# Grouped bursts: scores between the two bursts of a head pair inside the up products

## The chip, the cores and the metric

The kernel runs on one core of a Trainium2 chip. The metric is the device time of one execution in microseconds (us), as the median of several executions.

## The reference, cut to what matters

Grouped-query attention over 8 batches of 384 rows (16 query heads, 4 key heads, head size 64), then a feed-forward block with a squared ReLU on the 3072 rows that the attention gives:

```python
scores = scale * np.matmul(q, k.transpose(0, 1, 3, 2))
attn = np.exp(scores - np.max(scores, axis=-1, keepdims=True))
attn = attn / (np.sum(attn, axis=-1, keepdims=True) + 1e-09)
x = np.matmul(attn, v)                 # heads side by side: 3072 x 1024
h = np.maximum(x @ w_in, 0.0)          # 1024 x 2048
out = (h * h) @ w_out                  # 2048 x 1024
```

## The kernel before, in words

The work goes batch by batch (384 rows each). TensorE is driven by one long list of pieces, and the program that writes the kernel plans the order of that list itself: a recorder (`Recorder`) keeps an estimated clock for each engine and an estimated end for each operation, and a planner loop asks at each step which pieces could start now. Each engine then executes its own list strictly in that order, with semaphore waits where operations depend on each other.

While the feed-forward block of one batch runs, the attention of the next batch is woven into it. Four kinds of pieces matter here:

- **Up pieces** (L927, in `zipped` and `strassen`, L836 and L868): from batch 2 on, x times w_in is done by a seven-product scheme (Strassen's, Winograd's form) on half-size blocks in fp16. A piece is eight matmuls of 192 columns, four in each 64-row half of the array. A batch has 28 units of four half pieces each. A finished unit is taken out of its PSUM bank (4 to 7) by DVE or ACT (L898 to L911), then scaled and squared by ACT and GpSimd (L812 to L824). In the planner an up piece is called "ffn".
- **Down pieces** (L971): h squared times w_out, in the same scheme; also "ffn". Their results leave PSUM by DVE or ACT into `y_sb` (L1126 to L1134, L1344) and go out on SP's DMA queue (L1351).
- **Pieces of scores** ("sc", `burst_small`, L464): two matmuls of 512 columns or four of 256 (L471), into one of the two pairs of banks (0, 1) and (2, 3), followed by one exponential on ACT (L481) into a slot of `expT`. There are 18 for a batch. From batch 3 on, `expT` has six slots for the twelve blocks of keys of a batch (L198), so later scores become allowed only when head pairs of outputs have been finished.
- **Outputs of a head pair** (`av_halves`, L525): eight pairs a batch, each in two bursts of 18 matmuls of 65 columns (L539), in one of the two pairs of banks. The first burst is "av", the second "av2". The second adds into the same banks from the opposite 64-row halves, and therefore waits for the first to complete; then DVE divides (L552, L554). After each second pair a DMA transpose on SP's queue (L559) turns the result into `xT`. When a batch has all of `xT`, DVE forms three sums and a difference (`sums`, L673, L682) that the up products need.

A stretch of up products and a stretch of down products alternate. The down stretch of batches 2, 4 and 6 is short (7 products), that of batches 3 and 5 long (14 products).

The changed loop (L1930 to L2030) plans everything from batch 2 on. In each round it makes a list of candidates, each a tuple of the estimated time at which it can start, a priority (lower goes first), its kind, and a flag that says whether its spacing is kept. Inside the up products (`inside`) the flag of outputs is set when at least `AV_IN` = 4 up pieces have passed since the last burst of either kind, and that of scores when `SC_LATE` = 2 pieces (for the next batch) or `SC_IN` = 8 pieces (for the one after) have passed since the last scores. Outside, one piece is enough. Then it picks:

```python
ready = [x for x in cand if x[3] and x[0] <= now] or [x for x in cand if x[0] <= now]
what = min(ready, key=lambda x: x[1]) if ready else min(cand)
```

So among the candidates that can start now, those whose flag is set come first; if there are none, any that can start now fills the gap; and if there is none either, the earliest is taken. An up piece always has its flag set. `upkeep` (L1697) places the work of the other engines between the pieces: loads, transposes, evictions, sums.

Of the kernel before, what the change touches and what calls it, by code (L numbers as in the profile page):

```python
# [171 lines left out]
def bass_gqa_attention__then__ffn_squared_relu_kernel(  # L172
# [32 lines left out]
    R = Recorder(nc)  # L205
# [1415 lines left out]
    ff = dict(b=0, tiles=list(range(EARLY, NFC)), now=[], down=downs(0), carry=None)  # L1621
# [41 lines left out]
    av_open = []  # L1663
    margin = 0.5
    since, AMONG = 9, 2
    AV_IN, SC_LATE, SC_IN = 4, 2, 8
    load_pieces, dma_at, pe_last, LOAD_GAP, TURN_GAP = [], [0.0], [], 2.0, 3.5

    BLOCK, EDGE = 128, 51
# [106 lines left out]
    while ff["b"] < SB:  # L1776
        now = R.clock["tensor"]
# [4 lines left out]
        cand = []  # L1782
        wait = 0.1 if split else 0.0
        if turn_q:
            b, g, w = turn_q[0]
# [5 lines left out]
        if av_q and len(av_open) < 1 + on_halves(av_q[0][0] - 1):  # L1791
            b, c = av_q[0]
# [12 lines left out]
        if sc_q:  # L1805
            b, u = sc_q[0]
# [15 lines left out]
            if ok:  # L1822
# [3 lines left out]
                t = max(R.when(reads=reads) + 1.5 * (b == 2 and u < 9), R.when(writes=[("bank", base + i) for i in range(2)]))  # L1826
                cand.append((t, 4 if beside or loose and b > SB else 2.5 if loose else 0, "sc"))
        early_banks[:] = [i for i in ((6, 7, 0, 1, 2, 3) if sc_q and sc_q[0] == (1, 0) else (6, 7)) if i not in held]
        for n, lane in enumerate(lanes):
            chunks, need, banks, _ = lane[0]  # L1830
            if x_done[0] >= chunks:
                t = R.when(reads=need)
                if banks is not None:
                    if not banks:
                        continue
                    t = max(t, open_bank(banks))
# [4 lines left out]
        if f_head is not None:  # L1841
            chunks, need, banks, piece, *swap = f_head
            if x_done[ff["b"]] >= chunks and not (held and banks and held & set(banks) and isinstance(banks, list)):
                t = max([R.when(reads=need)] + [x() for x in swap])
                if banks:
                    t = max(t, max(open_bank([i]) for i in banks) if isinstance(banks, list) else open_bank(banks))
# [10 lines left out]
        if not cand:  # L1857
            b = next_sum()
# [68 lines left out]
                R.clock["tensor"] += 0.0 if on_halves(ff["b"] - 1) else 0.1  # L1927
            ff_take(split)

    since_av, since_sc = 9, 9  # L1930
    while ff["now"] or ff["tiles"] or ff["down"]:
        now = R.clock["tensor"]
        upkeep(now)
# [12 lines left out]
                    t = max(t, max(open_bank([i]) for i in banks) if isinstance(banks, list) else open_bank(banks))  # L1946
                cand.append((t, 5, "ffn", True))
        if av_open:
            cand.append((R.ops[av_open[0][3]]["end"], 0, "av2", since_av >= (AV_IN if inside else 1)))
        if av_q and len(av_open) < 2:  # L1950
            b, c = av_q[0]
            needs = {(b, c // 2 * NJ + j, 3 * (c % 2) + t) for j in range(NJ) for t in range(3)}
            places = [p for p in PAIRS if not held & set(p)]
            if needs <= scored and b in measured and b <= ff["b"] + 1 and b - NXT not in tail_open and places:
                place = min(places, key=lambda p: max(open_bank([i]) for i in p))
                t = max(max(open_bank([i]) for i in place), R.when(reads=av_reads(b, c)))
                cand.append((t, 1, "av", since_av >= (AV_IN if inside else 1)))
        if spread_q:
            pair = min((p for p in PAIRS if not held & set(p)), key=lambda p: max(open_bank([i]) for i in p), default=None)
            if pair:  # L1960
# [1 line left out]
        if sc_q:  # L1962
            b, u = sc_q[0]
            pieces = later[u]
            tiles = {(b, x, t) for x, c0, n in pieces for t in range(c0 // 128, (c0 + n) // 128)}
            bases = [i for i in (0, 2) if not held & {i, i + 1}]
            if (turned >= b or (b, max(x for _, x, _ in tiles) // (NU // 2)) in turned_h) and b <= ff["b"] + 2 and not (inside and len(ff["now"]) <= 10 and b > ff["b"] + 1) and (b != LEAN or pairs >= 8 * b) and pairs // 2 * NJ + SLOTS[b] > b * NU + max(x for _, x, _ in tiles) and bases:
                base = min(bases, key=lambda i: max(open_bank([i + x]) for x in range(2)))
                t = max(R.when(reads=[r for p in pieces for r in score_reads(b, *p)]) + 3.0 * (b > SB + 1), max(open_bank([base + i]) for i in range(2)))
                cand.append((t, 3, "sc", since_sc >= ((SC_LATE if b == ff["b"] + 1 else SC_IN) if inside else 1)))  # L1970
        if not cand:
            if force():
                continue
# [10 lines left out]
        ready = [x for x in cand if x[3] and x[0] <= now] or [x for x in cand if x[0] <= now]  # L1984
        what = min(ready, key=lambda x: x[1]) if ready else min(cand)
        since_av = 0 if what[2] in ("av", "av2") else since_av + (what[2] == "ffn")
        since_sc = 0 if what[2] == "sc" else since_sc + (what[2] == "ffn")
        if what[2] == "av":
            b, c = av_q.pop(0)
# [56 lines left out]
```

## Time and profile before

| | |
|---|---|
| median of 3 runs | 394.03 us (393.51 to 394.4) |
| the profiled execution, its own time | 394.68 us |
| its span in the trace | 392.6 us |
| TensorE matmuls busy | 386.4 us (98%) |
| TensorE weight loads busy | 305.3 us (78%) |
| VectorE (DVE) busy | 309.0 us (79%) |
| ScalarE (ACT) busy | 272.1 us (69%) |
| GpSimd (POOL) busy | 143.6 us (37%) |

The profile is one execution; times in it are counted from the start of its span. PE is TensorE's matmul row, PEld its weight loads, which run beside the matmuls. Matmuls overlap, so the distance between two starts, and not the length of one, is what a matmul costs. A line of a group names the line of the kernel, the engine, the operation, output and inputs, the count, busy time and mean length, and the idle time ahead of it with what ended it. In the rows of waits the numbers are the total in us, the count and the longest. In the rows of windows they are the length of the stretch, and for each engine its busy time and (x) its number of instructions, then TensorE's clock, the share of the DMA engines and GB/s.

In this trace the five up stretches with outputs woven in run from about 128.9, 166.9, 218.2, 257.2 and 308.7 us; the short down stretches begin at about 152, 243 and 333 us.

### The profile page before, as it was taken

What the parts mean: (1) busy time and instruction counts of PE and PEld (TensorE: products, weight loads), DVE (VectorE), ACT (ScalarE), POOL (GpSimd) and SP (SyncE); (2) the same over time, 40 slices, a digit from 0 to 9 for tenths busy, and PEclk for the clock granted to TensorE, in tenths of its full rate; (3) what the DMA queues carried; (4) which work ended last, traced back from release to release, by engine and by line L of the source; (5) the groups of instructions that cost most, each with busy time, mean ns of one, the idle gap of its engine ahead of it and who ended that gap; (6) DMA issues with size and microseconds to landing.
All of it is one profiled execution on the core that took longest, in us unless ns stands there. A gap on an engine that the chain in (4) does not pass through costs nothing. (4 is left out here: it accounts for less than half of the span.)

```text
span 392.6 us, 15577 instructions
## 1 busy us (share of the span) xinstructions
PE 386.4 (98%) x6987; PEld 305.3 (78%) x6990; DVE 309.0 (79%) x645; ACT 272.1 (69%) x397; POOL 143.6 (37%) x167
## 2 busy tenths in 40 slices
PE   8899999999999999999999999999999999999997
PEld 6565674455555899899988999899988899899643
DVE  4589788899989988888886678797885688856642
ACT  6848998789845897868882587878782297435511
POOL 7765420044002563466422154526401145225210
PEclk9999999999999999999999999999999999999999
DMA  9999999996339875884798316877722222120013
GB/s 176 179 197 154 206 202 178 160 258 103 42 78 131 182 104 75 126 161 79 99 133 172 120 25 83 123 139 94 69 64 86 102 46 23 48 83 4 28 68 122
DMA packets 95635, 44.40 MB, mean 113 GB/s; under 512 B 75984, under 2 KB 89552, under 8 KB 95568
## 3 DMA queue, kind: packets, MB, share of 16 engines
q0 software_dynamic: 36672, 17.44, 35.7%
q1 hardware_dynamic: 58080, 25.39, 32.2%
q8 instruction: 55, 0.90, 1.0%
q10 hardware_dynamic: 816, 0.57, 0.5%
q14 instruction: 12, 0.10, 0.1%
HBM read 35.65 MB, written 12.58 MB: 123 GB/s over the span
## 5 line engine op out<-in xcount | busy, mean ns | idle before, releaser
L481 ACT ACTIVATE expT<-ps 128x1024 bf16<-128x1024 f32 (+1 forms) x124 | 121.1, 1015 | 24.7 <-PE ps L471 24.3
L971 PE MATMUL ps<-w_out_sb,h2T 64*128 64x512 f16 x512 | 94.5, 376 | 0.0
L927 PE MATMUL ps<-xT,w_in_sb 64*128 64x192 f16 x1152 | 84.3, 243 | 0.3 <-DVE y_sb L1134 0.2
L927 PEld LDWEIGHTS ps<-xT,w_in_sb 64*128 64x128 f16 x1152 | 70.5, 94 | 3.0 <-PE ps L927 0.7
L824 POOL TENSOR_TENSOR h2T<-hr 128x384 f16<-128x384 f32 x55 | 44.8, 835 | 53.7 <-ACT hr L812 53.6
L927 PE MATMUL ps<-s_all,wx 64*128 64x192 f16 x768 | 51.8, 242 | 0.0
L471 PE MATMUL ps<-qT,kT 64*128 64x256 bf16 (+2 forms) x336 | 51.3, 323 | 0.5 <-DVE qT L442 0.2
L812 ACT ACTIVATE hr<-hr,bits 128x384 f32<-128x384 f32 x72 | 42.6, 608 | 11.1 <-DVE hr L911 10.7
L971 PE MATMUL ps<-area,xT 64*128 64x512 f16 x256 | 50.1, 376 | 0.0
L971 PEld LDWEIGHTS ps<-w_out_sb,h2T 64*128 64x128 f16 (+1 forms) x512 | 38.0, 94 | 14.8 <-DVE hr L898 0.4
L911 DVE TENSOR_TENSOR hr<-ps,hr 128x384 f32<-128x384 f32 x72 | 39.3, 555 | 8.4 <-PE ps L927 5.1
L927 PEld LDWEIGHTS ps<-s_all,wx 64*128 64x128 f16 x768 | 43.7, 94 | 1.2
L1126 ACT ACTIVATE y_sb<-ps,bits 128x512 f32<-128x512 f32 (+2 forms) x23 | 15.3, 669 | 40.4 <-PE ps L971 31.2
L1134 DVE SCALAR_TENSOR_TENSOR y_sb<-ps,bits,y_sb 128x512 f32<-128x512 f32 (+1 forms) x36 | 26.3, 745 | 21.1 <-PE ps L971 13.2
L635 PE MATMUL ps<-xT,w_in_sb 64*128 64x384 bf16 x448 | 41.6, 323 | 0.4 <-DMA w_in_sb<-in_moe_w_in_dram 0.2
L539 PE MATMUL ps<-v_aug,expT 64*128 64x65 bf16 x1680 | 41.8, 190 | 0.1
L539 PEld LDWEIGHTS ps<-v_aug,expT 64*128 64x128 bf16 x1680 | 38.4, 94 | 1.9 <-DVE o_sb L554 0.3
L635 PEld LDWEIGHTS ps<-xT,w_in_sb 64*128 64x128 bf16 x448 | 22.2, 94 | 15.0 <-issue 1.3
L927 PE MATMUL ps<-xT,wx 64*128 64x192 f16 x384 | 32.6, 242 | 0.0
L927 PE MATMUL ps<-s_all,w_in_sb 64*128 64x192 f16 x384 | 32.5, 242 | 0.0
L971 PE MATMUL ps<-area,h2T 64*128 64x512 f16 x128 | 31.9, 376 | 0.0
L903 ACT COPY hr<-ps 128x384 f32<-128x384 f32 x33 | 15.5, 481 | 23.3 <-PE ps L927 22.7
(152 smaller groups left out, 746.1 us busy)
## 6 DMA issues: line engine op xcount, KB each, us to landing
out_dram<-y_sb SPq DMA_DIRECT2D x45, 256.0 KB, 2.5
w_in_sb<-in_moe_w_in_dram POOLq DMA_DIRECT2D x8, 512.0 KB, 15.1
w_out_sb<-in_moe_w_out_dram POOLq DMA_DIRECT2D x4, 1024.0 KB, 30.9
q_st<-in_q_dram POOLq DMA_DIRECT2D x19, 192.0 KB, 5.1
q_st<-in_q_dram POOLq DMA_DIRECT2D x4, 384.0 KB, 25.5
k_st<-in_k_dram POOLq DMA_DIRECT2D x6, 192.0 KB, 4.5
k_st<-in_v_dram POOLq DMA_DIRECT2D x5, 192.0 KB, 4.8
wx<-in_q_dram POOLq DMA_DIRECT2D x2, 384.0 KB, 6.7
```

The source lines that it names most:

```text
L471: mm = pe.matmul(ps[:, base + x, m * wide:(m + 1) * wide], kT[at(b)][64 * x:64 * x + 64, u, :], q_cols(b, u // NJ, x, c0, c0 + wide))
L481: R.add("scalar", lambda e: e.activation(dst, src, AF.Exp, scale=0.125), reads=keys, writes=[("expT", slot(b, u), t) for u, _, _ in pieces ...
L539: m = pe.matmul(ps[:, p[x], n * DP:n * DP + D + 1], w, v_aug[b % 2][r, g * NJ + j, 0:D + 1], start=(n + j + y == 0), stop=(n + j + y == 2 ...
L635: m = pe.matmul(bank(4 + xs[x])[:, 0:S], w_in_sb[r, kc, c * 128:(c + 1) * 128], xT[b % NXT][r, kc, :], start=(phase < 2 and kc == 0), stop ...
L812: R.add("scalar", lambda e, val=val, to=to: e.activation(val, val, AF.Relu, scale=to), reads=[("hr", r)] + by, writes=[("hr", r)], cost=0. ...
L824: n = R.add(eng, lambda e, dst=dst, two=two: e.tensor_tensor(dst, two, two, ALU.mult), reads=[("hr", r)], writes=keys, cost=0.77 if other ...
L903: R.add("scalar", lambda e: e.copy(hr[r][:, :], src), reads=[("bank", at)], writes=[("hr", r)], cost=0.45, after=hr_read.pop(r, ()))
L911: R.add("vector", lambda e: e.tensor_tensor(hr[r][:, :], src, hr[r][:, :], ALU.add), reads=[("bank", at), ("hr", r)], writes=[("hr", r)], ...
L927: return lambda pe: pe.matmul(bank(at)[:, f * h:f * h + h], w[r, kc, c:c + 128], m[r, kc, :], start=(prod in (1, 5, 2) and y + f + kc == 0 ...
L971: return lambda pe: pe.matmul(bank(p.at)[:, 0:512], p.a(k, r), p.w(k, r), start=start, stop=stop, skip_group_check=True)
L1126: R.add(eng, lambda e: e.activation(y_sb[y][:, c0:c1], bank(at)[:, c0:c1], AF.Copy, scale=gs[g]) if eng == "scalar" else e.tensor_scalar(y ...
L1134: R.add("vector", lambda e: e.scalar_tensor_tensor(y_sb[z][:, c0:c1], bank(at)[:, c0:c1], gs[g], y_sb[y][:, c0:c1], ALU.mult, ALU.add), re ...
```

## The change

Four edits in the planner loop, all for the time inside the up products:

- A first burst may start when five up pieces (`AV_GROUP`) have passed since the last burst, instead of four. A second burst keeps four, except in a group (below).
- The spacing of scores of the next batch is six up pieces instead of two.
- `lately` holds the kinds of the last two pieces. Right after a first burst, a piece of scores has its flag set whatever the spacing, if ACT's estimated clock is at most 1.2 us ahead, and it has priority over all else, if it can start within 0.3 us.
- Right after a first burst and a piece of scores, the second burst has its flag set whatever the spacing, and its estimated start is put 0.1 us earlier.

The computation stays the same; only the order of the pieces changes, and with it what the planner places between them.

```diff
-    AV_IN, SC_LATE, SC_IN = 4, 2, 8
+    AV_IN, AV_GROUP, SC_LATE, SC_IN = 4, 5, 6, 8
...
-    since_av, since_sc = 9, 9
+    since_av, since_sc, lately = 9, 9, ["ffn", "ffn"]
...
-            cand.append((R.ops[av_open[0][3]]["end"], 0, "av2", since_av >= (AV_IN if inside else 1)))
+            cand.append((R.ops[av_open[0][3]]["end"] - 0.1 * (lately == ["av", "sc"]), 0, "av2",
+                         since_av >= (AV_IN if inside else 1) or inside and lately == ["av", "sc"]))
...
-                cand.append((t, 1, "av", since_av >= (AV_IN if inside else 1)))
+                cand.append((t, 1, "av", since_av >= (AV_GROUP if inside else 1)))
...
-                cand.append((t, 3, "sc", since_sc >= ((SC_LATE if b == ff["b"] + 1 else SC_IN) if inside else 1)))
+                cand.append((t, -1 if lately[-1] == "av" and t <= now + 0.3 else 3, "sc", inside and lately[-1] == "av" and R.clock["scalar"] <= now + 1.2 or since_sc >= ((SC_LATE if b == ff["b"] + 1 else SC_IN) if inside else 1)))
...
         what = min(ready, key=lambda x: x[1]) if ready else min(cand)
         since_av = 0 if what[2] in ("av", "av2") else since_av + (what[2] == "ffn")
+        lately = [lately[-1], what[2]]
```

## The prediction

> **What bounds the kernel now.** I read the page's head first, then the clock row, then the waits of TensorE over the stretch in which the changed loop orders the work (128 to 346 us), then its timeline.
>
> ```profile
> span 392.6 us, 15577 instructions
> PE 386.4 (98%) x6987; PEld 305.3 (78%) x6990; DVE 309.0 (79%) x645; ACT 272.1 (69%) x397; POOL 143.6 (37%) x167
> ...
> PEclk9999999999999999999999999999999999999999
> ```
>
> ```profile
> PEld ps L927 <- PE ps L927: 0.4, 1, 0.4
> PEld ps L927 <- DVE y_sb L1344: 0.3, 1, 0.3
> PE ps L927 <- DVE y_sb L1134: 0.2, 1, 0.2
> PEld ps L539 <- PE ps L539: 0.2, 1, 0.2
> PEld ps L539 <- ACT expT L481: 0.2, 1, 0.2
> ```
>
> TensorE is busy for 386.4 of 392.6 us at full clock. In the 218 us that the change can reorder, all its waits together are at most 1.3 us (0.4 + 0.3 + 0.2 + 0.2 + 0.2). So TensorE's own work sets the time there, and a new order can gain only what the old one costs: those waits, and whatever a boundary between two kinds of pieces costs. The next rows show the price of a boundary (columns: start, length, engine, line, count). L927 is an up piece, L471 a piece of scores, L539 a burst of outputs.
>
> ```profile
> 231.31 0.45 PE L539 MATMUL ps<-v_aug,expT 64*128 64x65 bf16 x18
> 231.58 0.24 PE L927 MATMUL ps<-xT,wx 64*128 64x192 f16 x1
> ...
> 234.72 0.45 PE L539 MATMUL ps<-v_aug,expT 64*128 64x65 bf16 x18
> 235.00 0.39 PE L471 MATMUL ps<-qT,kT 64*128 64x512 bf16 x2
> 235.21 0.24 PE L927 MATMUL ps<-xT,w_in_sb 64*128 64x192 f16 x1
> ```
>
> ```profile
> 168.13 0.51 PE L927 MATMUL ps<-xT,w_in_sb 64*128 64x192 f16 x8
> 168.45 0.40 PE L471 MATMUL ps<-qT,kT 64*128 64x256 bf16 x4
> 168.67 0.46 PE L539 MATMUL ps<-v_aug,expT 64*128 64x65 bf16 x18
> 168.96 0.42 PE L927 MATMUL ps<-xT,w_in_sb 64*128 64x192 f16 x6
> ```
>
> From start to next start, a burst takes 0.27 before an up piece (231.58 - 231.31), 0.28 before scores (235.00 - 234.72), and 0.29 behind scores (168.96 - 168.67). Scores take 0.21 to 0.22 (235.21 - 235.00, 168.67 - 168.45), and one up piece of eight matmuls 0.32 (168.45 - 168.13). Whatever stands beside a piece, its length agrees within 0.02 us. A boundary is all but free.
>
> **The change part by part.** No instruction is added or removed; only the order changes, and only while up pieces are left in the list.
>
> ```profile
> 128.90:345.70 216.80, 35.36 (x1404) 32.37 (x1404) 1.00 0.57 96
> ```
>
> ```profile
> 218.20:242.90 24.70, 6.57 (x270) 6.07 (x271) 1.00 0.36 70
> 242.90:257.20 14.30, 0.55 (x18) 0.46 (x18) 1.00 0.88 126
> ```
>
> These are the windows of L539: 1404 matmuls, 18 to a burst, are 78 bursts in the five up stretches and what follows them; in the up stretch of batch 4, 15 bursts (270 / 18) stand inside and the sixteenth just behind it. So before, eight head pairs already fit a stretch, with at least four up pieces after most bursts. A stretch has 56 half units, three of which go with the down products ahead of it: some 53 pieces are left.
>
> *The group.* After a first burst, a ready piece of scores goes ahead of everything, and then the second burst. The second burst waits for the first to complete (they add into the same banks from opposite row halves). The price of that wait uncovered is in the trace once, where the planner put the two bursts back to back:
>
> ```profile
> 134.23 0.95 PE L539 MATMUL ps<-v_aug,expT 64*128 64x65 bf16 x36
> ```
>
> ```profile
> 134.15 0.39 PEld L539 LDWEIGHTS ps<-v_aug,expT 64*128 64x128 bf16 x18
> 134.73 0.33 PEld L539 LDWEIGHTS ps<-v_aug,expT 64*128 64x128 bf16 x18 [0.19 <-PE ps L539]
> ```
>
> The second burst's first weights came 0.50 us after the first burst began (134.73 - 134.23). With scores between, TensorE is free again after 0.28 + 0.21 = 0.49 us, so 0.01 us of wait is left; before, four up pieces (1.3 us) hid it whole. While the second burst waits, every up piece queued behind it on TensorE waits too. Walking the new rules through the up stretch of batch 4, groups form at pairs 2 to 6: pairs 0 and 1 come before any scores are allowed (their slots open only when both are done), and at pair 7 no scores are left. Five groups in each of five stretches are 25 x 0.01 = 0.25 us, bounded by 0 below and, if the first weight load of 0.09 us (the LDWEIGHTS row of the page's PEld groups gives 94 ns) is exposed each time, by 25 x 0.03 above, taking a third of it. I take +0.2.
>
> ```profile
> L481 ACT ACTIVATE expT<-ps 128x1024 bf16<-128x1024 f32 (+1 forms) x124 | 121.1, 1015 | 24.7 <-PE ps L471 24.3
> ...
> L539 PEld LDWEIGHTS ps<-v_aug,expT 64*128 64x128 bf16 x1680 | 38.4, 94 | 1.9 <-DVE o_sb L554 0.3
> ```
>
> *The adjacent pair at 134.23.* It was a gap filler, because no up piece was ready. In the new order that pair is likely to have scores between its bursts: -0.2 us. Bounds 0 and -0.22.
>
> *Five pieces between groups, six between late scores.* The scores that each stretch has to place are counted by the exponentials (windows of L481):
>
> ```profile
> 128.90:152.10 23.20, 13.06 (x13) 1.00 0.63 107
> ...
> 218.20:242.90 24.70, 9.07 (x9) 1.00 0.36 70
> ```
>
> The walk through the batch 4 stretch, in up pieces: burst, 1, two bursts, 4, burst, scores, 5, group (2), 5, group (3), 6, scores, 4 (the exponential of 1.015 us must end before pair 4 may start), group (4), 6, scores, 5, group (5), 6, scores, 5, group (6), 5, burst, 4, burst. That is 56 pieces where some 53 are to be had. So all nine pieces of scores still stand inside, and the last burst slips by some three pieces into the down products behind, where one piece of spacing is enough: it ends some 0.3 us later than now. In the stretch of batch 2, which has thirteen pieces of scores to place, I count, by the same rules, two pieces of scores and one more burst spilling, and the last pair about 1 us later. TensorE does the same work either way: 0.0 us, as long as what hangs on the last pair has room.
>
> *What moves with it.* Each group brings one exponential on ACT (1.015 us) and a reciprocal and a multiply on DVE (0.18 + 0.56, rows below) earlier or later by up to six pieces (2 us). TensorE is covered because an up bank is reopened some three pieces (1 us) after it closed. The transposes of the outputs on SP's queue follow each second pair; of them only the last is on a path, the one that leads into the next up stretch:
>
> ```profile
> 243.89 0.18 DVE L552 RECIPROCAL bits<-ps 128x6 f32<-128x6 f32 x1
> 244.11 0.56 DVE L554 TENSOR_TENSOR o_sb<-ps,bits 128x384 f16<-128x384 f32 x1
> ...
> 249.92 0.75 DVE L1134 SCALAR_TENSOR_TENSOR y_sb<-ps,bits,y_sb 128x512 f32<-128x512 f32 x1 [0.38 <-PE ps L971]
> 251.47 0.29 DVE L713 TENSOR_REDUCE bits<-ps 128x1 f32<-128x128 f32 x1 [0.80 <-PE ps L709]
> ...
> 252.06 2.00 DVE L682 TENSOR_TENSOR s_all<-xT 128x768 f16<-128x768 f16 x1
> ...
> 257.03 0.75 DVE L1134 SCALAR_TENSOR_TENSOR y_sb<-ps,bits,y_sb 128x512 f32<-128x512 f32 x1
> ```
>
> ```profile
> 244.70 1.37 SPq L559 DMA_TRANSPOSE xT<-o_sb  x1
> ```
>
> ```profile
> 257.35 0.33 PE L927 MATMUL ps<-xT,w_in_sb 64*128 64x192 f16 x2
> 257.92 0.24 PE L927 MATMUL ps<-xT,w_in_sb 64*128 64x192 f16 x1 [0.24 <-DVE y_sb L1134]
> ```
>
> Behind the short down stretch of batch 4 the path is already tight: outputs at 244.67, transpose issued at 244.70, sums on DVE from 252.06, then L1134, which frees a bank for which TensorE waits until 257.92. A last pair that comes 0.3 us later costs between 0 (DVE stands idle for 0.38 and 0.80 us ahead of the sums, so there is slack before them) and 0.3 (all of it passed on to L1134); I take 0, because the idle time is the longer.
>
> **Sum.** +0.2 - 0.2 + 0.0 = 0.0. The profiled execution took 394.68 us (its span 392.6 and 2.1 around it); it would stay at 394.7. It lies 0.65 above the median of the three runs shown, 394.03, so the forecast for the median is **394.0 us**. About 0.2% (0.8 us) is what a measurement of this kernel can tell from no change.
>
> **The rivals.**
>
> *A burst gets cheaper in the group (faster).* If weights of the second burst were loaded under the scores' matmuls, the burst would be bound by its columns alone: 9 pairs x 65 / 192 x 0.08 us (an up pair is a quarter of 0.32) = 0.24 us instead of 0.28. Over 25 groups, both bursts, that is 50 x 0.04 = 2.0 us: 392.0. Against it: the one burst that already stands behind scores took 0.29, not less. The same place holds the boundary: 10 fewer excursions a stretch, 50 in all, at no more than 0.01 us each, are 0.5 us, not enough by itself. The Trainium skill, page "TensorE: Matmul & The Clock Gate", section "The mechanism", says that TensorE has a reorder window of 64 and pulls weight loads ahead of running matmuls where the row groups do not conflict. By that rule the scores' matmuls would hide the loads; the row at 168.67 does not bear it out as a gain, since the loads are already hidden in the bursts beside up pieces.
>
> *The last pairs come late (slower).* The place is the short down stretch of batches 2, 4 and 6. If scores are often not ready at the moment the first burst ends, no group forms, the second burst waits four pieces and the next pair five: nine pieces a pair instead of eight. Then pairs 6 and 7 spill as four bursts among down pieces, ending about 4 x (0.28 + 0.43) = 2.8 us after the up stretch (a down piece of four matmuls at 0.11 each, 166.44 - 166.33 below), sums and L1134 follow 2.8 us later, while three more bursts in the down stretch put the next up stretch off by 0.84. The wait at 257.92 grows by 2.0 us; it decides from the first 0.1 us there, since TensorE already waits. With less in the other two short stretches the time is some 396.0, from 394.9 to 397. For it: ACT is busy in the batch 2 stretch nearly without pause, and the path has no room at 257.9. Against it: the walk gives 0.3 us, and a list with no ready up piece is filled with outputs as now.
>
> ```profile
> 166.33 0.38 PE L971 MATMUL ps<-w_out_sb,xT 64*128 64x512 f16 x1
> 166.44 0.38 PE L971 MATMUL ps<-area,h2T 64*128 64x512 f16 x1
> ```
>
> ```profile
> 128.90:152.10 23.20, 23.11 (x647) 21.72 (x648) 20.54 (x41) 21.15 (x32) 14.78 (x17) 1.00 0.63 107
> ```
>
> (In that row of the windows ACT is busy 21.15 of 23.20 us, the number ahead of "(x32)".)
>
> *The change does little of what it says.* A group needs scores whose bank is free at the very moment the first burst ends. Where it is not, up pieces follow as now. If so at half the pairs, the self-wait halves and the rest stays: 394.0 again, so long as the rival above does not set in.
>
> **How the numbers follow.** The forecast 58%, the change doing little 8%, the late last pairs 24%, the cheaper bursts or waits that vanish 10%. The first two stay within 0.2% (393.2 to 394.8): same 66%, slower 24%, faster 10%. The range reaches from 393.1, below which only a part of the 10% lies, to 395.9, which takes in the self-wait's upper bound (0.75), a stall of about 1.1 us, and half of the slow rival. The likeliest case's own range is 393.3 to 394.8.
>
> **What would show it.** Right: up pieces in runs of 40 matmuls or more, bursts and scores as 18, 2 or 4, 18 without a break, with the second burst's weights waiting 0.01 us or so; the sum of TensorE's waits between 128 and 346 us within 0.5 of 1.3; the up stretches as long as now. Wrong towards slower: a longer wait on L1134 or on the sums at the starts of up stretches, or waits of L471 on the exponential. Wrong towards faster: bursts of 0.25 us instead of 0.28, or the waits listed above gone.

## The result, and the profile after

The changed kernel takes **399.87 us** (median of 4 runs, 397.34 to 400.56); the kernel before took 394.16 us beside it (4 runs, 393.51 to 394.4). The ratio is **1.0129, with a 95% interval of 1.0108 to 1.015**: slower by some 5.7 us, outside the predicted range. The profiled execution took 399.23 us.

The page of the changed kernel answers to the first rows of the prediction:

```profile
span 397.4 us, 15578 instructions
...
PE 389.7 (98%) x6987; PEld 298.7 (75%) x6990; DVE 309.4 (78%) x642; ACT 273.2 (69%) x397; POOL 148.2 (37%) x170
...
PEclk9999999999999999989999999999999999999999
```

TensorE's share looks as before, 98%, in a span 4.8 us longer. DVE has three operations less and GpSimd three more: the order of the pieces also changes what the planner gives to these two. Two marks betray what happened: its busy time is 3.3 us longer for the same 6987 matmuls, and the eighteenth slice of the clock row, 168.9 to 178.8 us, has an 8. The waits of TensorE between 128 and 350 us, first its matmuls, then its weight loads:

```profile
PE ps L927 <- DVE y_sb L1134: 2.5, 1, 2.5
```

```profile
PEld ps L539 <- PE ps L539: 1.9, 12, 0.2
PEld ps L971 <- DVE bits L552: 0.9, 1, 0.9
```

Where all waits together had been at most 1.3 us, a single one is now 2.5 us. The first row of the weight loads is the one that the prediction was busy with: the second burst waiting for the first, 12 times, 0.2 us at most, and for the greater part beside matmuls that still run.

To see where the time is lost I cut both traces where the first up piece of a batch starts on TensorE (U) and where, behind its last up piece, the eighth matmul of down products starts (D), and compare the lengths. The column "batch 4" runs from U4 to U5, the column U5 to D5, and "rest" from there to the end. Before, the boundaries lie at U2 126.93, D2 154.04, U3 166.87, D3 193.82, U4 218.20, U5 257.19 us. Differences to before, in us, for the changed kernel and for the experiments told below:

| kernel | opening | U2 | D2 | U3 | D3 | batch 4 | U5 | rest | span |
|---|---|---|---|---|---|---|---|---|---|
| changed | -0.60 | -0.15 | +0.92 | **+4.35** | +0.20 | +0.13 | -0.20 | +0.12 | +4.76 |
| old_rules_batch2 | -1.07 | 0.00 | 0.00 | -0.17 | +0.36 | +0.13 | -0.21 | +0.11 | -0.85 |
| new_rules_batch2_only | -0.55 | +1.48 | +0.91 | +4.48 | +0.11 | 0.00 | -0.05 | -0.01 | +6.37 |
| last_pair_late_24 | -0.88 | +0.39 | +0.47 | +2.44 | +0.11 | 0.00 | -0.05 | 0.00 | +2.48 |
| last_pair_late_34 | -1.34 | +0.01 | +0.75 | +3.82 | +0.11 | -0.01 | -0.05 | -0.01 | +3.28 |
| copy_after_sums | -0.73 | +1.78 | +0.91 | +1.16 | +0.20 | +0.13 | -0.21 | +0.12 | +3.36 |
| both_copies_moved | -0.55 | +0.15 | +0.91 | +1.16 | +0.20 | +0.13 | -0.21 | +0.10 | +1.88 |
| copies_apart | -0.81 | -0.16 | +0.91 | +0.99 | +0.20 | +0.13 | -0.21 | +0.12 | +1.17 |
| groups_old_spacing | -0.39 | +0.37 | +0.84 | +0.21 | +0.33 | +0.03 | +3.78 | 0.00 | +5.18 |
| spacing_without_groups | -0.50 | -0.07 | +2.66 | +1.06 | +0.81 | +0.05 | -1.19 | +3.79 | +6.62 |

The changed loop does not plan the opening, and it still differs by up to 1.3 us between these executions, so the later columns carry the argument. **All of the loss lies behind the batch 2 stretch, 0.92 us in its down products and 4.35 us in the up products of batch 3.** Behind U3 the same rules change each column by 0.2 us at most, up or down.

Here is what reaches the up products of batch 3. First TensorE behind the batch 2 stretch, in the kernel before and in the changed one:

```profile
154.16 0.45 PE L539 MATMUL ps<-v_aug,expT 64*128 64x65 bf16 x15
...
154.87 0.46 PE L539 MATMUL ps<-v_aug,expT 64*128 64x65 bf16 x15
```

```profile
154.10 0.37 PE L971 MATMUL ps<-w_out_sb,h2T 64*128 64x512 f16 x1 [0.43 <-DVE bits L552]
...
155.83 0.46 PE L539 MATMUL ps<-v_aug,expT 64*128 64x65 bf16 x18
156.11 0.39 PE L471 MATMUL ps<-qT,kT 64*128 64x512 bf16 x2
156.76 0.46 PE L539 MATMUL ps<-v_aug,expT 64*128 64x65 bf16 x18
```

The last burst of batch 3 starts at 156.76 instead of 154.87: counted from the last up piece, it stands behind 28 matmuls of down products, where it stood behind 12. Its head pair needs the last piece of scores of that batch, and that piece now comes at 152.32, behind the up pieces, where it stood inside them at 150.30. ACT has scalings and squares to do and takes its exponential last:

```profile
154.28 1.00 ACT L481 ACTIVATE expT<-ps 128x1024 bf16<-128x1024 f32 x1
```

The first burst of the pair follows it, at 155.83. This is read from the order and the times; no run moved that piece of scores alone. Now DVE, SP's queue and GpSimd in the kernel before (L554 divides, L559 is the transpose, L682 are the sums, L1134 frees a bank of TensorE, L1242 is a copy of half-size blocks on GpSimd):

```profile
155.69 0.56 DVE L554 TENSOR_TENSOR o_sb<-ps,bits 128x384 f16<-128x384 f32 x1
...
163.36 0.55 DVE L682 TENSOR_TENSOR s_all<-xT 128x768 f16<-128x768 f16 x1
163.95 0.56 DVE L682 TENSOR_TENSOR s_all<-s_all,xT 128x768 f16<-128x768 f16 x1
...
165.64 0.75 DVE L1134 SCALAR_TENSOR_TENSOR y_sb<-ps,bits,y_sb 128x512 f32<-128x512 f32 x1
```

```profile
156.27 1.21 SPq L559 DMA_TRANSPOSE xT<-o_sb  x1
```

```profile
167.69 1.88 POOL L1242 COPY area<-h2T 128x2048 f16<-128x2048 f16 x1
```

and the same three in the changed kernel:

```profile
158.32 0.56 DVE L554 TENSOR_TENSOR o_sb<-ps,bits 128x384 f16<-128x384 f32 x1
...
165.50 0.75 DVE L1134 SCALAR_TENSOR_TENSOR y_sb<-ps,bits,y_sb 128x512 f32<-128x512 f32 x1 [0.83 <-PE ps L971]
...
166.78 1.23 DVE L682 TENSOR_TENSOR s_all<-xT 128x768 f16<-128x768 f16 x1
168.04 2.13 DVE L682 TENSOR_TENSOR s_all<-s_all,xT 128x768 f16<-128x768 f16 x1
...
171.70 1.40 DVE L1134 SCALAR_TENSOR_TENSOR y_sb<-ps,bits,y_sb 128x512 f32<-128x512 f32 x2
```

```profile
158.91 1.21 SPq L559 DMA_TRANSPOSE xT<-o_sb  x1
```

```profile
166.33 1.26 POOL L1169 TENSOR_TENSOR y_sb<-y_sb 128x512 f32<-128x512 f32 x1 [0.97 <-DVE y_sb L1134]
167.55 2.21 POOL L1242 COPY area<-h2T 128x2048 f16<-128x2048 f16 x1
```

Outputs and transpose come 2.6 us later. The sums come 3.4 us later, as they now stand in DVE's list behind an L1134 that waits 0.83 us for TensorE. And they have become long: the first takes 1.23 us instead of 0.55, the second 2.13 instead of 0.56. They ran into two operations of GpSimd which before came when the sums were over: the first into L1169, the second into the copy L1242. The second sum ends at 170.17 (168.04 + 2.13), 0.41 us after the copy does (167.55 + 2.21 = 169.76). Behind the sums, L1134 opens TensorE's bank:

```profile
168.74 1.27 PE L539 MATMUL ps<-v_aug,expT 64*128 64x65 bf16 x54
172.50 2.19 PE L927 MATMUL ps<-xT,w_in_sb 64*128 64x192 f16 x32 [2.50 <-DVE y_sb L1134]
```

The planner had nothing but outputs left to fill with, three bursts in a row, and then TensorE stands for 2.50 us. The windows of the stretch behind that wait (the number behind POOL's is the granted clock):

```profile
168.70:172.50 3.80, 1.24 (x60) 0.99 (x54) 3.73 (x8) 1.63 (x2) 1.06 (x1) 1.00 0.65 126
172.50:174.50 2.00, 2.00 (x34) 1.91 (x36) 1.93 (x5) 0.88 (x2) 0.00 (x0) 0.66 0.00 0
174.50:176.70 2.20, 2.20 (x42) 1.94 (x38) 1.02 (x2) 0.07 (x1) 0.00 (x0) 0.54 0.46 88
```

The clock falls after the wait. In narrower windows it is 0.75 in 173.00 to 173.25, exactly 0.50 from there to 176.50, and 0.96 in the half microsecond behind: some 3.4 us at half speed. Work lost to it: 2.00 x (1 - 0.66) + 2.20 x (1 - 0.54) = 1.7 us. So the 4.35 us of U3 are 2.50 of wait, 1.7 of clock and a remainder of 0.15. Each run's own mean clock tells the same: a stretch of 3.4 us at half speed in 397 us makes it 0.996, and of the four runs of the changed kernel two have 0.996 (399.23 and 400.51 us) and two 1.000 (397.34 and 400.56 us).

The Trainium skill, page "SBUF — State Buffer", section "SBUF: two separate sides", says that DVE and GpSimd share one pair of ports as an exclusive lock: an operation of DVE with two SBUF inputs and one of GpSimd that reads SBUF do not run beside each other, and the loser waits for the whole instruction. The second sum, which ends just behind the copy, agrees with it. The same skill, page "TensorE: Matmul & The Clock Gate", section "Why this matters for your kernels", asks for no idle gaps over about 3 us; here a gap of 2.50 us was enough, so the measurement decides. The length of the slow stretch agrees with the free-running window of 3413 ns that Part 1 of that page gives.

### The profile page after: what moved, and what is told of

It reads as the page before. It is cut to its first block, busy times and chain, and to the rows that moved or that the text cites. A ratio compares the mean times of both kernels' runs of the same rounds, so it can differ in the third digit from the quotient of the medians.

```text
span 397.4 us, 15578 instructions
## 1 busy us (share of the span) xinstructions
PE 389.7 (98%) x6987; PEld 298.7 (75%) x6990; DVE 309.4 (78%) x642; ACT 273.2 (69%) x397; POOL 148.2 (37%) x170
## 4 chain that ended last, share of the span: by engine, by line
PE 94%; DVE 3%; ACT 2%; issue 0%
PE ps L971 30%; PE ps L927 28%; PE ps L635 9%; PE ps L471 7%; PE ps L539 7%; PE ps L1319 5%; PE ps L1026 2%; PE ps L497 2%; ACT expT L481 2%; PE ps L598 1%; PE ps L1406 1%; DVE s_all L682 1%; PE ps L573 1%; DVE hr L648 0%; DVE y_sb L1134 0%
## 5 line engine op out<-in xcount | busy, mean ns | idle before, releaser
L927 PE MATMUL ps<-xT,w_in_sb 64*128 64x192 f16 x1152 | 83.4, 245 | 2.6 <-DVE y_sb L1134 2.5
L927 PEld LDWEIGHTS ps<-xT,w_in_sb 64*128 64x128 f16 x1152 | 71.3, 95 | 5.9 <-DVE y_sb L1134 2.6
L824 POOL TENSOR_TENSOR h2T<-hr 128x384 f16<-128x384 f32 x56 | 45.7, 835 | 54.7 <-ACT hr L812 54.2
L927 PE MATMUL ps<-s_all,wx 64*128 64x192 f16 x768 | 50.4, 244 | 0.0
L971 PEld LDWEIGHTS ps<-w_out_sb,h2T 64*128 64x128 f16 (+1 forms) x512 | 36.8, 94 | 17.7 <-DVE bits L552 0.9
L812 ACT ACTIVATE hr<-hr,bits 128x384 f32<-128x384 f32 x69 | 40.5, 607 | 10.6 <-DVE hr L911 10.2
L1134 DVE SCALAR_TENSOR_TENSOR y_sb<-ps,bits,y_sb 128x512 f32<-128x512 f32 (+1 forms) x36 | 26.3, 745 | 20.3 <-PE ps L971 12.9
L539 PEld LDWEIGHTS ps<-v_aug,expT 64*128 64x128 bf16 x1680 | 36.2, 94 | 5.3 <-PE ps L539 1.9
L1126 ACT ACTIVATE y_sb<-ps,bits 128x512 f32<-128x512 f32 (+2 forms) x21 | 13.9, 666 | 37.9 <-PE ps L971 27.7
L903 ACT COPY hr<-ps 128x384 f32<-128x384 f32 x41 | 19.3, 480 | 23.3 <-PE ps L927 22.9
```

The lines of the kernel that those rows point to most:

```text
L539: m = pe.matmul(ps[:, p[x], n * DP:n * DP + D + 1], w, v_aug[b % 2][r, g * NJ + j, 0:D + 1], start=(n + j + y == 0), stop=(n + j + y == 2 ...
L812: R.add("scalar", lambda e, val=val, to=to: e.activation(val, val, AF.Relu, scale=to), reads=[("hr", r)] + by, writes=[("hr", r)], cost=0. ...
L824: n = R.add(eng, lambda e, dst=dst, two=two: e.tensor_tensor(dst, two, two, ALU.mult), reads=[("hr", r)], writes=keys, cost=0.77 if other ...
L903: R.add("scalar", lambda e: e.copy(hr[r][:, :], src), reads=[("bank", at)], writes=[("hr", r)], cost=0.45, after=hr_read.pop(r, ()))
L927: return lambda pe: pe.matmul(bank(at)[:, f * h:f * h + h], w[r, kc, c:c + 128], m[r, kc, :], start=(prod in (1, 5, 2) and y + f + kc == 0 ...
L971: return lambda pe: pe.matmul(bank(p.at)[:, 0:512], p.a(k, r), p.w(k, r), start=start, stop=stop, skip_group_check=True)
```

## The experiments

The theory after this reading: the new order of the **batch 2 stretch** brings the last pair of batch 3 late, the sums that hang on it meet GpSimd's copy, TensorE waits and is then slowed. The rivals: the groups or the wider spacing cost by themselves, in each stretch; or the lateness alone costs it, without the copy.

**old_rules_batch2.** The changed kernel with the old rules in the batch 2 stretch only (SB is 2).

```diff
-                cand.append((t, 1, "av", since_av >= (AV_GROUP if inside else 1)))
+                cand.append((t, 1, "av", since_av >= ((AV_GROUP if ff["b"] != SB else AV_IN) if inside else 1)))
...
-        lately = [lately[-1], what[2]]
+        lately = [lately[-1], what[2]] if ff["b"] != SB else ["ffn", "ffn"]
```

(and `SC_LATE` replaced by 2 there in the same way).

> The changed kernel, but with the old rules (spacing of 4 and 2, no groups) while the up products of batch 2 run; groups and wider spacing stay in the stretches of batches 3 to 6. Theory (the loss is the last head pair of batch 3, which the new order of the batch 2 stretch puts 2.4 us later, and what hangs on it): all of the loss goes, 393.8 us, from 393.3 to 394.5, and no wait on L1134 at the start of the batch 3 stretch. Rival (a group costs by itself, wherever it stands): four of five stretches keep it, 398 us or more.

Measured: 394.05 us (10 runs, 393.46 to 395.34) beside 394.0 of before; ratio 1.0001, 0.9989 to 1.0013. The whole loss is gone, as expected. Its waits hold the self-waits still:

```profile
PEld ps L539 <- PE ps L539: 1.8, 11, 0.2
```

So groups and spacing in four of the five stretches cost nothing that this measurement can tell (its interval is 0.5 us either way), and bring nothing either.

**new_rules_batch2_only.** The opposite: `==` in place of `!=`.

> The kernel before, with the new rules only while the up products of batch 2 run. Theory (late last pair of batch 3): the whole loss stays, 398 to 400.5 us, with a wait of 2 us or more on L1134 at the start of the batch 3 stretch and a lower granted clock behind it. Rival (a group costs by itself): one stretch of five, 395.2 us or less.

Measured: 400.84 us (4 runs, 400.02 to 401.83); ratio 1.0168, 1.0143 to 1.0192. All of the loss, and a little more, 0.3 us above the expected range: D2 +0.91, U3 +4.48 as in the changed kernel, and U2 +1.48, a second collision that is told under copy_after_sums.

**last_pair_late_24** and **last_pair_late_34.** The kernel before, in which the first burst of the last pair of batch 3 may only be placed when the up products are over and at most 16 entries (in the second, 14) of the planner's down list are left, so that its second burst stands behind 24 or 34 matmuls of down products.

```diff
-            if needs <= scored and b in measured and ...
+            if not ((b, c) == (LATE, 7) and (inside or len(ff["down"]) > 16)) and needs <= scored and b in measured and ...
```

> The kernel before, old rules everywhere, but the last head pair of batch 3 is held back: its second burst stands behind 24 matmuls of down products instead of 12 (in the changed kernel 28). No group, no new spacing. Theory (the lateness of this one pair makes the loss): the sums on DVE start some 1.5 to 3 us later, meet GpSimd's copy, and the time is 396 to 399 us, with a wait on L1134 at the start of the batch 3 stretch. Rival (the groups or the order inside the up products make the loss): 394 us.

> As the run with 24, but the second burst of the last pair of batch 3 stands behind 34 matmuls. Theory: more than with 24, by about the 1.1 us of ten matmuls if the path has no room left: 397.5 to 401 us, with a wait of over 2 us and a lower granted clock behind it. Rival: 394 us.

Measured: 398.41 us (4 runs, 397.27 to 399.12), ratio 1.0108, 1.0088 to 1.0129; and 398.32 us (4 runs, 396.94 to 398.7), ratio 1.0094, 1.0069 to 1.0119. The old rules with nothing but a late last pair lose 4 us of the 5.7. The later one does not lose more, against what I expected: in both a sum that stands beside the copy ends 0.4 us after it (170.06 behind 169.65, and 168.77 behind 168.35), so the copy sets its end. DVE and TensorE of last_pair_late_24:

```profile
157.13 0.56 DVE L554 TENSOR_TENSOR o_sb<-ps,bits 128x384 f16<-128x384 f32 x1
...
167.82 2.24 DVE L682 TENSOR_TENSOR xT<-xT 128x768 f16<-128x768 f16 x1
```

```profile
171.93 1.49 PE L927 MATMUL ps<-xT,w_in_sb 64*128 64x192 f16 x32 [2.23 <-DVE y_sb L1134]
```

The outputs are 1.4 us late (155.69 before), a sum takes 2.24 us beside the copy (167.44 to 169.65 here), and TensorE waits 2.23 us. In this execution the clock stayed at 1.00 behind the wait; in the profiled one of last_pair_late_34 it fell after a shorter wait, at 171.81:

```profile
171.10 2.11 PE L927 MATMUL ps<-xT,w_in_sb 64*128 64x192 f16 x32 [1.96 <-DVE y_sb L1134]
```

So near 2 us it is not the length alone that decides. The clock that the traces record shows what does. The three stretches at half speed (173.12 to 176.54 in the changed kernel, 175.25 to 178.67 in new_rules_batch2_only, 171.81 to 175.22 here) last 3.413 us each, and they begin 49, 50 and 49 times 3.413 us after the clock of that execution had first come to full. Counted off in such windows from there, the wait of 1.96 us lies inside one window, and so does that of 2.50 us in the changed kernel. The wait of 2.23 us, from 169.70 to 171.93, lies across an edge at 170.32 (the clock came to full at 6.48, and 6.48 + 48 x 3.4133 = 170.32). Windows ahead of the fall in the changed kernel and in last_pair_late_34, then the two of last_pair_late_24 (the second number is TensorE's busy time):

```profile
169.71:173.12 3.41, 0.91 (x34) 0.78 (x28) 3.34 (x9) 0.69 (x2) 0.05 (x1) 1.00 0.26 79
```

```profile
168.40:171.81 3.41, 1.38 (x49) 1.09 (x43) 3.33 (x9) 0.95 (x2) 0.00 (x0) 1.00 0.05 17
```

```profile
166.91:170.32 3.41, 2.72 (x98) 2.48 (x94) 3.41 (x4) 3.07 (x3) 2.74 (x2) 1.00 0.95 167
170.32:173.73 3.41, 1.80 (x50) 1.75 (x52) 3.27 (x10) 0.96 (x2) 0.00 (x0) 1.00 0.00 1
```

The clock fell behind windows with 0.91, 1.06 (new_rules_batch2_only) and 1.38 us of work, and not behind those with 1.54 (spacing_without_groups, 171.10 to 174.51), 1.72 (copy_after_sums, 130.96 to 134.38) and 1.80. So the same wait can cost 1.7 us more or nothing, by where it falls. The single runs fit this: three of the four of each late pair have a mean clock of 0.996, at 398.07 to 399.12 us, and one has 1.000, at 397.27 and 396.94 us.

**copy_after_sums.** The changed kernel with GpSimd's copy L1242 held until the last of the four L682 is done. It acts on all three of these copies, beside the sums of batches 3, 5 and 7.

```diff
-            keys = [("h2T", c, 1) for c in range(NFC)] + [("DS", b, "A", n, x) for n in (2, 3) for x in range(2)]
+            keys = [("h2T", c, 1) for c in range(NFC)] + [("DS", b, "A", n, x) for n in (2, 3) for x in range(2)] + [("S", 2)]
```

> The changed kernel, with one more dependency: GpSimd's copy at L1242 waits for the last of DVE's four sums (L682). TensorE's order stays as in the changed kernel. Theory (the late sums meet the copy, and two of them take 1.2 and 2.1 us instead of 0.55): the sums take 2.2 us again, L1134 comes 2.2 us earlier, TensorE waits 0.7 us or less in place of 2.5, the clock stays at 1.00: 395 to 396 us. Rival (the late landing of the transpose alone makes it): the wait stays above 2 us, 398.5 us or more.

Measured: 397.06 us (7 runs, 395.54 to 397.96); ratio 1.006, 1.0042 to 1.0078. Half of the loss goes, with the late last pair still there. The first sum still takes 1.23 us, beside L1169, which the edit does not move. Sums, copy and TensorE:

```profile
169.85 0.56 DVE L682 TENSOR_TENSOR s_all<-s_all,xT 128x768 f16<-128x768 f16 x1
```

```profile
171.41 1.89 POOL L1242 COPY area<-h2T 128x2048 f16<-128x2048 f16 x1 [2.01 <-DVE s_all L682]
```

```profile
172.74 1.49 PE L927 MATMUL ps<-xT,w_in_sb 64*128 64x192 f16 x32 [0.93 <-DVE y_sb L1134]
```

The second sum is back at 0.56, the wait at 0.93 instead of 2.50, and the clock behind it stays at 1.00: U3 is +1.16 instead of +4.35. The copy and what it set off, wait and clock, were 3.2 us of that stretch. But the time came out above the 395 to 396 that I had in mind, because of U2, +1.78. There a second pair of operations meets, DVE's L1281 (f16, two SBUF inputs) and GpSimd's copy of the keys L361:

```profile
130.03 2.90 DVE L1281 TENSOR_TENSOR w_out_sb<-w_out_sb 128x1024 f16<-128x1024 f16 x1
```

```profile
130.89 1.48 POOL L361 COPY k_dup<-k_st 128x1536 bf16<-128x1536 bf16 x1
```

```profile
133.68 0.39 PE L471 MATMUL ps<-qT,kT 64*128 64x256 bf16 x4 [1.63 <-DVE o_sb L554]
```

L1281 ends 0.56 us after the copy (130.03 + 2.90 = 132.93; 130.89 + 1.48 = 132.37), L554 (at 133.06) is held up behind it, and scores wait 1.63 us for the banks. In the profile of the changed kernel the two just miss each other. In new_rules_batch2_only they meet as here (L1281 2.60 us). This meeting and the clock are two things seen here that differ from run to run. The changed kernel's runs spread from 397.34 to 400.56 us; only one of them was profiled, so how much of the spread is theirs is not shown.

**both_copies_moved** was to hold L361 until all four L1281 are done, in addition.

> The changed kernel with two more dependencies: GpSimd's copy at L1242 waits for DVE's last sum, and its copy at L361 for batch 4 waits for DVE's last operation at L1281. The orders of TensorE and DVE are those of the changed kernel. Theory (the late pair costs about 2.2 us by itself, the rest of the loss is DVE held up beside GpSimd's two copies and the clock): 395.3 to 396.5 us, all runs within about 1 us of each other, L1281 at 0.7 us each but for the one under other work, clock 1.00. Rival (the spread of the changed kernel comes from elsewhere): 397 us as with one copy moved, runs 2 us apart.

Measured: 397.28 us (4 runs, 396.47 to 397.9); ratio 1.0083, 1.0054 to 1.0112. The expectation failed because the edit did nothing: at the moment L361 is put in the list, the fourth L1281 is not in it yet, so there is nothing to wait for, and L361 still ran at 131.45. In its profile L361 and L1281 miss each other (U2 +0.15). As an order it is copy_after_sums again.

**copies_apart.** copy_after_sums, and L361 waits for the first L1281.

```diff
-              reads=[("k_st", at(b)) if b else ("k_f32", g) for g in range(g0, g1)],
+              reads=[("k_st", at(b)) if b else ("k_f32", g) for g in range(g0, g1)] + [("w2t", 0)] * (b == LATE + 1),
```

> The changed kernel, with GpSimd's copy of batch 3 (L1242) behind the three sums, as in copy_after_sums, and GpSimd's first copy of the keys of that batch (L361) held back until the first of the four L1281 of DVE is done. The whole computation stays. It asks whether L361 is what makes L1281 long in the batch 2 stretch. Theory (the two hold each other up where they meet): L1281 takes about 0.7 us each as long as no L361 runs, the scores of that stretch do not wait 1.6 us on L554, the stretch is within 0.5 us of before's, and what is left of the loss is some 2 us behind it (0.9 down stretch, 1.2 next up stretch): 395.8 to 396.8 us, single times less than 1 us apart. Rival 1 (L1281 is long for another reason, such as GpSimd's issues of DMAs): L1281 still takes over 1.5 us, the stretch is 1.5 us longer, 397 to 398.5 us. Rival 2 (the held copy only moves the meeting to a later L1281): one later L1281 is long, and it costs nothing as in the kernel before, or up to 1.5 us if scores hang on it.

Measured: 395.63 us (5 runs, 395.11 to 395.95); ratio 1.0038, 1.0023 to 1.0052. DVE, GpSimd and TensorE in it:

```profile
129.94 0.68 DVE L1281 TENSOR_TENSOR w_out_sb<-w_out_sb 128x1024 f16<-128x1024 f16 x1
130.76 0.56 DVE L554 TENSOR_TENSOR o_sb<-ps,bits 128x384 f16<-128x384 f32 x1
```

```profile
130.85 1.48 POOL L361 COPY k_dup<-k_st 128x1536 bf16<-128x1536 bf16 x1
```

```profile
170.55 1.50 PE L927 MATMUL ps<-xT,w_in_sb 64*128 64x192 f16 x32 [0.89 <-DVE y_sb L1134]
```

L1281 takes 0.68 us, the stretch is as long as before (U2 -0.16), and the single times lie within 0.84 us. L554, which reads PSUM, takes its usual 0.56 beside the copy. What is left is D2 +0.91 and U3 +0.99, some 1.5 us in the median, 0.2 us below the expected range. It is not lateness alone: the third of the four L682 still takes 1.63 us, beside GpSimd's L1169 (167.06 beside 166.76), 1.1 us more than alone. Both rivals fall: no L1281 is long.

**before_copy_after_sums** and **old_batch2_copy_after_sums** put the later copy L1242 into the kernel before, and into the changed kernel with the old rules in batch 2.

> The kernel before with GpSimd's copy at L1242 made to wait for the last of DVE's four sums; the order on every engine is the same. Theory (the copy slows the sum at 252.06 to 2.00 us and so makes TensorE wait 0.4 us at 257.9): that wait goes, 393.4 to 393.8 us. Rival (the copy was harmless, or is then late itself): 394.0 us or more.

> The changed kernel with the old rules in the batch 2 stretch, and GpSimd's copy at L1242 waiting for DVE's last sum. If the groups in the other stretches are nearly free (+0.1 us each) and the copy's move takes away the wait at the start of the batch 5 stretch: 393.3 to 393.9 us, the same as the kernel before with the copy moved (393.5). If groups bring a gain of their own that the copy hid: below 393.2 us.

Measured: 393.47 us (12 runs, 393.1 to 395.25) beside 394.37, ratio 0.9989, 0.9973 to 1.0004; and 394.03 us (12 runs, 393.7 to 395.05), ratio 1.0001, 0.9988 to 1.0014. In the first, the copy of batch 5 no longer meets the sums of the kernel before, first GpSimd's row and then DVE's:

```profile
255.18 1.89 POOL L1242 COPY area<-h2T 128x2048 f16<-128x2048 f16 x1 [2.46 <-DVE s_all L682]
```

```profile
253.04 0.54 DVE L682 TENSOR_TENSOR s_all<-xT 128x768 f16<-128x768 f16 x1
```

The first sum took 2.00 us in the prediction's row at 252.06; now it takes 0.54, the wait at 257.92 is gone, and U5 is 0.40 us shorter. That is the fastest version found, and within what was expected, but the interval holds 1, so a gain is not shown. The groups add nothing to it: the second came out 0.1 us above its expected range.

**groups_old_spacing.** The changed kernel with groups, but the old spacings.

```diff
-    AV_IN, AV_GROUP, SC_LATE, SC_IN = 4, 5, 6, 8
+    AV_IN, AV_GROUP, SC_LATE, SC_IN = 4, 4, 2, 8
```

> The changed kernel with the old spacing (4 up pieces before a first burst, 2 before scores) and the groups kept. Theory (late last pair): the last burst of batch 3 stands behind 8 matmuls of down products instead of 28, so 393.8 to 394.8 us with no long wait on L1134. Rival (a group costs by itself): 397 us or more.

Measured: 399.83 us (4 runs, 399.54 to 400.66); ratio 1.0144, 1.0123 to 1.0165. The number that I expected failed, and the time came where the rival (a group costs by itself) had put it. But the loss is not spread over the groups: U3 is back to +0.21, so the place was right, D2 has +0.84, and one other stretch, U5, lost 3.78:

```profile
263.04 1.74 PE L539 MATMUL ps<-v_aug,expT 64*128 64x65 bf16 x72
267.33 0.24 PE L927 MATMUL ps<-s_all,wx 64*128 64x192 f16 x1 [1.59 <-issue]
```

Four bursts stand in a row there, each second one waiting uncovered for its first, and then TensorE stands for 1.59 us under "issue": nothing that the profile shows ended it. Together with shorter waits (0.29 and 0.34 us at matmuls of the same stretch) and two uncovered self-waits of about 0.2 each, this accounts for some 2.6 of the 3.8 us. What the 1.59 us were stays open. It does show that each such rule reorders five stretches, and that a stretch far from the one that was looked at can break.

**spacing_without_groups.** The changed kernel with the spacings, but no group ever formed.

```diff
-        lately = [lately[-1], what[2]]
+        lately = ["ffn", "ffn"]
```

> The changed kernel without the groups: a first burst waits for five up pieces and scores for six, but no piece of scores follows a first burst at once. In the batch 2 stretch three scores and four bursts are left over, and the last burst of batch 3 stands behind 56 matmuls of down products. Theory (late last pair, made by the spacing): the worst of all, 400 us or more. Rival (groups make the loss): 394 to 395 us.

Measured: 402.26 us (4 runs, 400.85 to 403.93); ratio 1.0202, 1.017 to 1.0233. The worst of all, as expected: scores pile up at the ends of the stretches and wait for the exponential:

```profile
PEld ps L471 <- ACT expT L481: 2.6, 4, 1.3
```

In this order part of the output's values came out changed, for a reason that stays open, so its time counts only as that of an order. It suggests that the wide spacing is what makes pieces late, and that the groups win back part of it. Its U3 lost 1.06 us only, with a wait of 1.9 us and no fall of the clock; the rest of its loss lies in D2 (+2.66) and at the end.

## Why the prediction was wrong

**The step that failed** is "Five pieces between groups, six between late scores", in its last two sentences: for the stretch of batch 2 it counted "two pieces of scores and one more burst spilling, and the last pair about 1 us later" and costed that at "0.0 us, as long as what hangs on the last pair has room". The runs showed a pair later by 2.6 us at its outputs, since a spilled piece of scores still had to go through its exponential ahead of it, and no room: undoing the rules in that one stretch takes the whole loss away (394.05), and making the pair late by itself in the kernel before costs 4 us (398.41).

Point by point:

- **What bounds the kernel.** Right: TensorE's work sets the time, and what was lost was lost as its waiting and its clock.
- **The group.** The mechanism was right, its price a little too low, its count too high: TensorE's list has 17 groups (3, 2, 4, 4 and 4 in the five stretches) where 25 were forecast. A group now takes, before scores and second burst:

```profile
129.67 0.45 PE L539 MATMUL ps<-v_aug,expT 64*128 64x65 bf16 x18
129.96 0.38 PE L471 MATMUL ps<-qT,kT 64*128 64x512 bf16 x2
130.19 0.46 PE L539 MATMUL ps<-v_aug,expT 64*128 64x65 bf16 x18
```

  The second burst begins 0.52 us after the first (130.19 - 129.67) where 0.50 was forecast. The wait is about 0.02 to 0.03, the upper bound rather than a third of it; that fits the +0.13 of batch 4 with its four groups, which is there with old rules in batch 2 as well. 17 times as much are 0.3 to 0.5 us, where +0.2 was taken.
- **The burst got no cheaper**: 0.29 before and behind scores. The rival of cheaper bursts is out.
- **What moves with it.** The path that I named, from the last pair over transpose and sums to L1134, was the right one; I looked for it at the wrong place. I walked through batch 4, where nine pieces of scores must be placed, and took its 257.92 as the tight spot. The batch 2 stretch has thirteen to place, and I let it go with one sentence. Even there the walk missed: the last burst came 24.77 us behind the first up piece (247.69 - 222.92), 0.1 us earlier than before (243.06 - 218.20 = 24.86) and not 0.3 later. So the wait at the tight spot went and U5 got 0.20 us shorter, which was not forecast.
- **The size.** The rival "the last pairs come late (slower)" had this mechanism, with 24% and +2.0 us at 257.92. It passed the lateness on one to one. What is left without the copy and the clock is the 1.5 us of copies_apart, in which a sum still takes 1.1 us too long beside L1169. The rest, about 4 us in the median (399.87 against 395.63), came of what the late sums ran into: GpSimd's copy, then the lowered clock, and at times L361 in the stretch before.
- **The price lay in a row that the prediction quotes**: the sum of 2.00 us at 252.06, beside 0.56 and 0.55 for its fellows. I used its start and did not ask why one of equal sums was four times as long. In the kernel before, GpSimd's row beside it is

```profile
251.71 1.92 POOL L1242 COPY area<-h2T 128x2048 f16<-128x2048 f16 x1
```

  The sums at 163.36 to 165.44 were short only because L1242 came at 167.69. So the cost of lateness has a step: nothing at first, and then the length of what the sums meet. Before, they ended at 165.44, L1169 began at 166.47 and the copy at 167.69; outputs 1.4 us late already met both (last_pair_late_24). Where the step begins below that was not tried.
- **D2, +0.91**, was not in the forecast: fewer outputs stand ahead of the first down products, so TensorE reaches them sooner and waits (0.43 us at the matmul of 154.10, 0.9 at its weight load; the profile names DVE's L552 here, and in copies_apart ACT's L820, which writes squares). That it waits for the last squares fits this; whether it is the whole +0.91 was not tried by itself.

## What to carry to other kernels

When a change moves work in time, follow each operation that hangs on it to its new place and ask what runs there on the other engines; a group of equal operations of which one is several times longer names a collision that others can move into. Walk the stretch with the most to place, not the one that looks tightest. A wait of the bounding engine can cost more than its length, and a reordering rule that acts in five stretches has to be priced in each.

## What the runs showed of the hardware

- **The clock after a wait.** It was granted at 1.00 or 0.50, in stretches of whole multiples of 3.413 us, counted from when it first came to full. A window of 3.413 us with at most 1.38 us of matmuls was followed by one at 0.50, which cost 1.7 us; one with 1.54 us or more was not. So waits of 1.96 and 2.50 us inside one window were followed by the fall, and one of 2.23 us across an edge was not, nor any quoted one of 0.89 to 1.63 us.
- **DVE beside GpSimd.** Operations of DVE with two f16 inputs in SBUF ended 0.4 to 0.6 us after the operation of GpSimd that they met: sums of 0.55 us took 1.03 to 2.61 (beside L1169 or the copy L1242), L1281 of 0.68 took 2.60 and 2.90 (beside the copy L361). One that reads PSUM kept its length beside L361 (L554, 0.56). L1281 and L361 met where their recorded starts were 0.56 and 0.86 us apart, and missed each other at 0.91, 0.94 and 1.05: a few hundredths decided over 1.6 us of TensorE.
